# Causal attention in pairs of heads: the order of its work made by a list scheduler in the builder

## The chip, the core and the metric

The kernel runs on one core of a Trainium2 chip. The metric is the device time of one execution in microseconds; the profile is of one more execution of the same program. The core's engines each run their own queue in order and wait for one another by semaphores: TensorE (PE, matmuls and transposes), VectorE (DVE), ScalarE (ACT), GpSimd (POOL), and SyncE (SP), which here issues transfers.

## What is computed

Attention with a causal mask over 2 x 12 heads of 448 positions, then a gated layer (gate, value, output weights, float64 in memory), then eight experts of which each token uses one.

```python
scores = scale * np.matmul(q, k.transpose(0, 1, 3, 2))      # 2 x 12 heads, 448 x 448, head_dim 64
scores = np.where(mask, -1000000000.0, scores)               # causal
scores = scores - np.max(scores, axis=-1, keepdims=True)
attn = np.exp(scores)
attn = attn / (np.sum(attn, axis=-1, keepdims=True) + 1e-09)
x = np.matmul(attn, v)            # -> (896 tokens, 768)
xn = x / rms * rms_g
out1 = (silu(xn @ w_gate) * (xn @ w_val)) @ w_out
...                               # routing, then relu(x @ w1[e]) @ w2[e] for each token's expert
```

## The kernel before

The heads are taken in twelve pairs (NP = 12, n is the pair), so that two heads of 64 fill 128 partitions. The 448 positions are four chunks of 112 queries; chunk c sees (c+1) x 112 keys, so chunk 3 is the widest. For one pair the work is:

- keys and queries are loaded (`load_qk`, SP), transposed on PE (`prep_t`, L225, four transposes each) and copied out of PSUM (`prep_out`, keys on DVE L233, queries on ACT L231);
- `score` (L256, mask added by L258): chunks 0 and 1 into one PSUM tile, chunk 2 and chunk 3 each into another; there are two such tiles (`pss`);
- `rowmax` (DVE, L264), then `expo` (ACT, L270, one exponential for each head and chunk, which also sums the row);
- `invert` (DVE, L275 and L276: add and reciprocal), then `norm`: chunks 0 to 2 are scaled on POOL (L283), chunk 3 on ACT, one instruction for each head (L286);
- `trans` (L301): 20 transposes of the scaled probabilities in six groups through two PSUM tiles (`pst`), each group copied out (three groups of 4 on DVE, one of 4 and two of 2 on ACT) into one tile `pt` per head;
- `pv` (L316): the value product into `ps_x`; `xevac` copies it out on DVE (L323); `xhigh` (ACT, L328) and `xlow` (DVE, L333) make the two parts of the rounded result, `square` (ACT, L344) and `add_square` (POOL, L351) the sum of squares.

The order is written by hand: a loop over n in L499 to L593 issues, in each turn, the scores and exponentials of pair n, the transposes of pair n-1 and the value product's end of pair n-2, so each engine's queue holds them in just this order. Between them stand `chore` steps: single operations of the conversion of the first gate and value weights (float64 bits to a high and a low float32 part: `f64_ops`, DVE L144, L147, L150, ACT L154, DVE or POOL L156), eight halves in all. In the last two turns `ahead` puts products of the first weight slice (f=0) between. `warm` (L199) is a matmul with zeros; it stands only at the start. After the attention the gate and value products run (`products`, L457 to L459): twelve slices f, two batch halves each, 36 matmuls for one half. A slice needs its converted weights; the program does four halves of conversion for each further slice.

Of the kernel before, what the change touches and what calls it, by code (L numbers as in the profile page):

```python
# [31 lines left out]
E = 8  # L32
# [8 lines left out]
def build(ctx, tc, q, k, v, w_gate, w_val, w_out, rms_g, emb, tau, w1, w2, out, dbg=None):  # L41
# [196 lines left out]
    def begin(n):  # L238
        st[n] = {
            "ps": {}, "pt": {},  # L240
            "p": a2.tile([CP, 2, 10 * CP], F32, name="p", tag="p", bufs=2),
            "nm": a2.tile([CP, NCH, 2], F32, name="nm", tag="nm", bufs=3),
            "sm": a2.tile([CP, NCH, 2], F32, name="sm", tag="sm", bufs=3),
        }

    def score(n, cs):

        e = st[n]
        bank = pss.tile([P, 2, 512], F32, name="ps_s", tag="s")
        qt, kt = parts[n, "qn"], parts[n, "kn"]  # L250
# [15 lines left out]
    def expo(n, c):  # L266
        e = st[n]
        w = (c + 1) * CP
        for h in range(2):
            A.activation(e["p"][:, h, COLS[c]:COLS[c] + w], e["ps"][c][:, h, :], AF.Exp, bias=e["nm"][:, c, h:h + 1],  # L270
                         accum_out=e["sm"][:, c, h:h + 1])
# [6 lines left out]
    def norm(n, c):  # L278

        e = st[n]  # L280
        d = e["p"][:, :, COLS[c]:COLS[c] + (c + 1) * CP]
        if c < NCH - 1:
            G.tensor_mul(d, d, e["sm"][:, c, :].unsqueeze(2).to_broadcast([CP, 2, (c + 1) * CP]))  # L283
        else:
            for h in range(2):
                A.mul(d[:, h, :], d[:, h, :], e["sm"][:, c, h:h + 1])  # L286


    TOFF = [0, 4 * CP, 8 * CP, 7 * CP]

    def trans(n, h, bank):
        e = st[n]
        if bank == 0:
            e["pt"][h] = a2.tile([CP, 10 * CP], F32, name="pt", tag="pt", bufs=4)
        ps = pst.tile([P, 512], F32, name="ps_t", tag="t")
        base = bank * 4 * CP
        w = 0
        for kc in ((0,), (1, 3), (2,))[bank]:
            for c in range(kc, NCH):
                o = TOFF[kc] - base + (c - kc) * CP  # L300
                T.transpose(ps[:CP, o:o + CP], e["p"][:, h, COLS[c] + kc * CP:COLS[c] + (kc + 1) * CP],  # L301
                            ident[:CP, :CP])
                w = max(w, o + CP)
        return e["pt"][h][:, base:base + w], ps[:CP, :w]
# [4 lines left out]
    def pv(n, kcs):  # L309
        vn = qkv[n, "vn"]  # L310
        if kcs[0] == 0:
            xps[n] = tbank() if n == NP - 1 else psx.tile([P, 512], F32, name="ps_x", tag="x")
        for kc in kcs:
            w = (NCH - kc) * CP
            for h in range(2):
                T.matmul(xps[n][h * D:(h + 1) * D, kc * CP:S], vn[:, kc, h * D:(h + 1) * D],  # L316
                         st[n]["pt"][h][:, TOFF[kc]:TOFF[kc] + w], start=kc == 0, stop=kc == NCH - 1)

    xraw = {}

    def xevac(n):
        xraw[n] = a2.tile([P, S], F32, name="xraw", tag="xraw", bufs=3)
        V.tensor_copy(xraw[n], xps.pop(n)[:, :S])  # L323

    def xhigh(n):

        b, j = divmod(n, NPAIR)
        A.mul(xh[:, j, b * S:(b + 1) * S], xraw[n], gT[:, j:j + 1])  # L328

    def xlow(n):  # L330
        b, j = divmod(n, NPAIR)
        cols = slice(b * S, (b + 1) * S)
# [25 lines left out]

    def means(b):

        ps = tbank()
        for c in range(NCH):
            T.matmul(ps[:CP, c:c + 1], xsq[b][:, c * CP:(c + 1) * CP], ones[:, :1], start=True, stop=True)
        rms[b] = a1.tile([CP, NCH], F32, name="r", tag="r", bufs=2)
        V.tensor_scalar(out=rms[b], in0=ps[:CP, :NCH], scalar1=1.0 / DM, scalar2=1e-6, op0=ALU.mult, op1=ALU.add)
# [115 lines left out]

    with tc.manual_schedule():
        load_qk(0)
        load_qk(1)
        load_qk(2)
# [3 lines left out]
        begin(0)  # L489
        first2 = pss.tile([P, 2, 512], F32, name="ps_s", tag="s")  # L490
        for x, (nm, engine) in enumerate((("kn", A), ("qn", V))):
            prep_out(*prep_t(0, nm, first2[:, x, :]), engine)
            warm(bank, 2)
        score(0, (0, 1))
        for nm, engine in (("kn", A), ("qn", V)):
            prep_out(*prep_t(1, nm, tbank()), engine)
            warm(bank, 2)
        load_v(0)
        for n in range(NP + 2):  # L499
# [35 lines left out]
            elif n:  # L535
                chore()
# [748 lines left out]
```

## Time and profile before

| | |
|---|---|
| median of 3 runs | 680.58 us (678.58 to 683.65) |
| profiled execution | 681.85 us, span 680.1 us |
| busy over the span | PE 628.8, DVE 468.6, ACT 315.3, POOL 202.2 us |
| attention | about 4 to 175 us |
| gate and value products | to 343.9 us |
| granted clock, 40 slices of 17 us, tenths | 9989777797999999999999999979989999999999 |

A busy share is time in which an engine has an instruction under way. Matmuls overlap, so PE's share says little of how near it is to its limit; the distance between starts says more. The granted clock is TensorE's alone: 1.00 is 2.4 GHz, 0.50 is 1.2 GHz, and a number between is a mean over a stretch. A wait is put down to the engine that ended it. In the waits and the timeline a name such as `xl` is the tile that is written; `p` are the probabilities, `nm` the negated maxima, `sm` the row sums and their reciprocals.

### The profile page before, as it was taken

What the parts mean: (1) busy time and instruction counts of PE and PEld (TensorE: products, weight loads), DVE (VectorE), ACT (ScalarE), POOL (GpSimd) and SP (SyncE); (2) the same over time, 40 slices, a digit from 0 to 9 for tenths busy, and PEclk for the clock granted to TensorE, in tenths of its full rate; (3) what the DMA queues carried; (4) which work ended last, traced back from release to release, by engine and by line L of the source; (5) the groups of instructions that cost most, each with busy time, mean ns of one, the idle gap of its engine ahead of it and who ended that gap; (6) DMA issues with size and microseconds to landing.
All of it is one profiled execution on the core that took longest, in us unless ns stands there. A gap on an engine that the chain in (4) does not pass through costs nothing. (4 is left out here: it accounts for less than half of the span.)

```text
span 680.1 us, 10132 instructions
## 1 busy us (share of the span) xinstructions
PE 628.8 (92%) x3402; PEld 513.0 (75%) x3402; DVE 468.6 (69%) x848; ACT 315.3 (46%) x669; POOL 202.2 (30%) x198
## 2 busy tenths in 40 slices
PE   8889788879999999999999999978989898999996
PEld 4545455546899999999999999846768687888885
DVE  3676664565899999999658999667348687841431
ACT  2766665665422323322253223567347687741321
POOL 2322323133254444444303444013213313331100
PEclk9989777797999999999999999979989999999999
DMA  7731411000365555555168226328739989981100
GB/s 177 179 92 28 104 38 38 1 24 24 95 178 161 171 160 167 148 177 160 51 213 282 86 74 206 117 71 274 286 103 313 368 306 348 332 309 48 48 24 10
DMA packets 83664, 101.85 MB, mean 150 GB/s; under 512 B 38368, under 2 KB 62944, under 8 KB 83570
## 3 DMA queue, kind: packets, MB, share of 16 engines
q1 hardware_dynamic: 80704, 90.12, 42.6%
q0 software_dynamic: 1856, 7.87, 3.3%
q10 hardware_dynamic: 1010, 2.76, 1.0%
q8 instruction: 42, 0.69, 0.4%
q14 instruction: 52, 0.43, 0.2%
HBM read 95.19 MB, written 6.71 MB: 150 GB/s over the span
## 5 line engine op out<-in xcount | busy, mean ns | idle before, releaser
L283 POOL TENSOR_TENSOR p<-p,sm 112x224 f32<-112x224 f32 (+2 forms) x36 | 34.7, 992 | 82.1 <-DVE sm L276 77.2
L256 PE MATMUL ps_s<-knt,qnt 64*112 64x112 f32 (+3 forms) x192 | 41.9, 520 | 18.6 <-ACT p L270 18.6
L156 POOL TENSOR_TENSOR wl<-t,wh 128x384 fp32r<-128x384 f32 x40 | 42.7, 1078 | 54.5 <-ACT wh L154 54.5
L150 DVE SCALAR_TENSOR_TENSOR t<-raw,t 128x384 int32<-128x384 int32 x72 | 57.1, 794 | 1.8
L796 PE MATMUL ps_y<-wo,hh 128*128 128x384 f32 x168 | 58.0, 345 | 0.0
L797 PE MATMUL ps_y<-wo,hh 128*128 128x384 f32 x168 | 56.6, 337 | 0.0
L798 PE MATMUL ps_y<-wo,hlo 128*128 128x384 f32 x168 | 56.6, 337 | 0.0
L270 ACT ACTIVATE p<-ps_s,nm 112x112 f32<-112x112 f32 (+3 forms) x96 | 46.1, 496 | 20.8 <-DVE nm L264 20.8
L457 PE MATMUL ps_g<-xh,wh 128*128 128x448 f32 x144 | 53.6, 372 | 0.0
L459 PE MATMUL ps_g<-xh,wl 128*128 128x448 f32 x144 | 53.5, 372 | 0.0
L458 PE MATMUL ps_g<-xl,wh 128*128 128x448 f32 x144 | 53.0, 368 | 0.0
L457 PE MATMUL ps_v<-xh,wh 128*128 128x448 f32 x144 | 52.8, 367 | 0.0
L459 PE MATMUL ps_v<-xh,wl 128*128 128x448 f32 x144 | 52.6, 365 | 0.0
L458 PE MATMUL ps_v<-xl,wh 128*128 128x448 f32 x144 | 52.6, 365 | 0.0
L147 DVE SCALAR_TENSOR_TENSOR t<-raw,t 128x384 int32<-128x384 int32 x72 | 50.4, 700 | 1.5
L154 ACT CAST wh<-t 128x384 fp32r<-128x384 f32 x48 | 24.7, 514 | 52.8 <-DVE t L150 44.3
L264 DVE TENSOR_REDUCE nm<-ps_s 112x2 f32<-112x224 f32 (+3 forms) x48 | 34.2, 733 | 17.5 <-PE ps_s L258 17.4
L301 PE MATMUL ps_t<-ident,p 112*112 112x112 f32 x240 | 41.2, 310 | 2.9 <-ACT pt L564 2.9
L256 PEld LDWEIGHTS ps_s<-knt,qnt 64*112 64x112 f32 x192 | 15.8, 206 | 33.4 <-ACT p L270 21.2
L144 DVE TENSOR_SCALAR t<-raw 128x384 int32<-128x384 int32 x72 | 38.0, 528 | 3.7 <-POOL wl L156 3.7
L156 POOL TENSOR_TENSOR wo<-t,wo 128x384 fp32r<-128x384 f32 x24 | 25.7, 1071 | 35.9 <-ACT wo L154 35.9
L301 PEld LDWEIGHTS ps_t<-ident,p 112*112 112x112 f32 x240 | 29.1, 160 | 7.7 <-ACT pt L564 5.7
(298 smaller groups left out, 1649.6 us busy)
## 6 DMA issues: line engine op xcount, KB each, us to landing
r<-in_moe_w SPq DMA_DIRECT2D x78, 384.0 KB, 5.3
hB<-in_moe_w SPq DMA_DIRECT2D x29, 384.0 KB, 3.4
raw<-in_moe_w_gate SPq DMA_DIRECT2D x24, 384.0 KB, 4.0
raw<-in_moe_w_val SPq DMA_DIRECT2D x24, 384.0 KB, 3.2
raw<-in_moe_w_out SPq DMA_DIRECT2D x24, 384.0 KB, 3.2
onehot<-in_moe_w SPq DMA_DIRECT2D x13, 384.0 KB
hA<-in_moe_w SPq DMA_DIRECT2D x8, 384.0 KB, 3.1
kn<-in_k SPq DMA_DIRECT2D x24, 112.0 KB, 2.5
```

The costliest lines, as they stand in the source:

```text
L147: V.scalar_tensor_tensor(out=t, in0=w[:, :, 1], scalar=-0x40000000, in1=t, op0=ALU.bitwise_and, op1=ALU.bitwise_or)
L150: V.scalar_tensor_tensor(out=t, in0=w[:, :, 0], scalar=29, in1=t, op0=ALU.logical_shift_right, op1=ALU.bitwise_or)
L156: low.tensor_sub(lo, f, hi.bitcast(F32))
L256: T.matmul(bank[:CP, h, o:o + w], qt[rows, c * CP:(c + 1) * CP], kt[rows, :w], start=True, stop=False)
L270: A.activation(e["p"][:, h, COLS[c]:COLS[c] + w], e["ps"][c][:, h, :], AF.Exp, bias=e["nm"][:, c, h:h + 1], accum_out=e["sm"][:, c, h:h + 1])
L301: T.transpose(ps[:CP, o:o + CP], e["p"][:, h, COLS[c] + kc * CP:COLS[c] + (kc + 1) * CP], ident[:CP, :CP])
L457: T.matmul(pg[:, :S], ah, bh, start=j == 0, stop=False)
L458: T.matmul(pg[:, :S], ah, bl, start=False, stop=False)
L459: T.matmul(pg[:, :S], al, bh, start=False, stop=j == NJ - 1)
L796: T.matmul(o, hh, bh, start=f == 0, stop=False)
L797: T.matmul(o, hh, bl, start=False, stop=False)
L798: T.matmul(o, hl, bh, start=False, stop=f == NF - 1)
```

## The change

The loop is replaced by a planner in the builder, `attention_order`. It lists every step of every pair as a node with an engine, a duration written in the code, the nodes that it needs, the buffers that it takes and gives, and a place from a table of constants. It then places one node after another: of the nodes that could start earliest on their engine (within 0.12) the one with the smallest place. The result is one list; the program issues it in that order, and where the plan leaves PE idle over 0.35 us it puts up to four `warm` matmuls into the PSUM tile that the next step writes. The conversions (`ch0` to `ch4`) and the early products (`gv`) are nodes too, with the largest places.

Besides the order: chunk 3 is scaled on POOL with the others; the first transposed group is copied by ACT for both heads (before by DVE for the first head), so ACT has four groups and DVE two; the transposed probabilities have a tile for each group (`pt0`, `pt1`, `pt2`, four of each) in place of one per head; `ps_x` is not copied out, `xhigh`, `square` and `xlow` read PSUM; scores and exponentials of chunk 1 come ahead of chunk 0, and chunk 3 ahead of chunk 2. Loads of keys and queries are issued four pairs ahead, of values five, the first of them in one row at the start.

```diff
     def norm(n, c):
 
         e = st[n]
-        d = e["p"][:, :, COLS[c]:COLS[c] + (c + 1) * CP]
-        if c < NCH - 1:
-            G.tensor_mul(d, d, e["sm"][:, c, :].unsqueeze(2).to_broadcast([CP, 2, (c + 1) * CP]))
-        else:
-            for h in range(2):
-                A.mul(d[:, h, :], d[:, h, :], e["sm"][:, c, h:h + 1])
+        w = (c + 1) * CP
+        d = e["p"][:, :, COLS[c]:COLS[c] + w]
+        G.tensor_mul(d, d, e["sm"][:, c, :].unsqueeze(2).to_broadcast([CP, 2, w]))
...
-    def xevac(n):
-        xraw[n] = a2.tile([P, S], F32, name="xraw", tag="xraw", bufs=3)
-        V.tensor_copy(xraw[n], xps.pop(n)[:, :S])
...
-        A.mul(xh[:, j, b * S:(b + 1) * S], xraw[n], gT[:, j:j + 1])
+        A.mul(xh[:, j, b * S:(b + 1) * S], xps[n][:, :S], gT[:, j:j + 1])
...
+    PLACES = dict(Pk=24, KE=12, Pq=19, QE=25, S01=10, S2=18, S3=-10, M0=21, E00=21, E01=5, M1=-7, E10=0, E11=-9,
...
+    def attention_order():
...
+            add("Pk", n, T, .385, [], ["pm", "kt"])
...
+            add("S01", n, T, 1.2, own("KE", "QE"), ["pss"])
+            add("S3", n, T, 1.08, own("S01"), ["pss"])
+            add("S2", n, T, .9, own("S3"), ["pss"], ["kt", "qt"])
...
+            for c, weight in enumerate((.56, .93, 1.6, 2.1)):
+                add(f"N{c}", n, G, weight, own("R1" if c < 3 else "R2"))
...
+                    add(f"C{h}{b}", n, V if b == 1 else A, (.53, .62, .34)[b], own(f"T{h}{b}"), gives=["pst"])
...
+            picks = []
+            for e, l in first.items():
+                t0 = min(l)[0]
+                picks.append(min((place[k], t, k) for t, k in l if t <= t0 + .12))
+            _, t, k = min(picks, key=lambda x: (x[1], x[0], x[2]))
...
-        for n in range(NP + 2):
-            cur, old = n < NP, 1 <= n <= NP
-            x = n - 2 if n >= 2 else None
...
+        for (kind, n), gap in attention_order():
+
+            fill = min(4, int((gap - .1) / .22)) if gap > .35 else 0
...
```

What this does to ACT's queue is seen in one pair in the middle of the attention. Before (L270 exponentials, `p,sm`; L538, L564, L572 copies of transposed groups; L286 scaling of chunk 3; L328 high part; L231 queries; L344 square):

```order
L270 ACTIVATE p,sm<-ps_s,nm 112x112 x2
L270 ACTIVATE p,sm<-ps_s,nm 112x224 x2
L270 ACTIVATE p,sm<-ps_s,nm 112x336 x2
L538 COPY pt<-ps_t 112x224
L270 ACTIVATE p,sm<-ps_s,nm 112x448 x2
L564 COPY pt<-ps_t 112x448
L286 ACTIVATE p<-p,sm 112x448 x2
L328 ACTIVATE xh<-xraw,gT 128x448
L572 COPY pt<-ps_t 112x224
L231 ACTIVATE qnt<-tq 128x448
L344 ACTIVATE sq<-xraw 128x448
```

In the changed program (L266 exponentials, L638 copies, L335 square, L320 high part; the number in `pt_` is that of a tile):

```order
L266 ACTIVATE p,sm<-ps_s,nm 112x224
L231 ACTIVATE qnt<-tq 128x448
L266 ACTIVATE p,sm<-ps_s,nm 112x224
L266 ACTIVATE p,sm<-ps_s,nm 112x112
L266 ACTIVATE p,sm<-ps_s,nm 112x448
L266 ACTIVATE p,sm<-ps_s,nm 112x112
L266 ACTIVATE p,sm<-ps_s,nm 112x448
L638 COPY pt_1005<-ps_t 112x224
L335 ACTIVATE sq<-ps_x 128x448
L320 ACTIVATE xh<-ps_x,gT 128x448
L638 COPY pt_1027<-ps_t 112x448
L266 ACTIVATE p,sm<-ps_s,nm 112x336
```

The scaling L286 is gone, square and high part stand behind one short copy, and the exponentials of the widest chunk (448) alternate with those of the narrowest (112), ahead of those of the 336 keys.

On DVE, before, from the copy of the value product on (L323), with L565 a transposed copy, L275 and L276 the sums and reciprocals of chunk 3, L333 the low part, L264 the maxima of the next pair:

```order
L323 COPY xraw<-ps_x 128x448
L233 COPY knt<-tq 128x448
L150 SCALAR_TENSOR_TENSOR t<-raw,t 128x384
L565 COPY pt<-ps_t 112x448
L275 TENSOR_SCALAR sm<-sm 112x2
L276 RECIPROCAL sm<-sm 112x2
L333 SCALAR_TENSOR_TENSOR xl<-xraw,gT,xh 128x448
L156 TENSOR_TENSOR wl<-t,wh 128x384
L264 TENSOR_REDUCE nm<-ps_s 112x2 x2
```

In the changed program (L638 transposed copies, L271 and L272 reciprocals, L259 maxima, L325 low part, L233 keys):

```order
L233 COPY knt<-tq 128x448
L638 COPY pt_1012<-ps_t 112x448
L271 TENSOR_SCALAR sm<-sm 112x2
L272 RECIPROCAL sm<-sm 112x2
L259 TENSOR_REDUCE nm<-ps_s 112x2
L638 COPY pt_1037<-ps_t 112x448
L325 SCALAR_TENSOR_TENSOR xl<-ps_x,gT,xh 128x448
L259 TENSOR_REDUCE nm<-ps_s 112x2
L271 TENSOR_SCALAR sm<-sm 112x6
L272 RECIPROCAL sm<-sm 112x6
L259 TENSOR_REDUCE nm<-ps_s 112x2
```

The copy out of PSUM is gone; one maximum stands between the reciprocals of chunk 3 (`112x2`) and the low part, and the reciprocals of the other chunks (`112x6`) come only after the next pair's first maximum.

On PE, before, the end of one turn: transposes of pair n-1, the last three parts of the value product of pair n-2, transposes, chunk-3 scores:

```order
L301 MATMUL ps_t<-ident,p 112x112 x4
L316 MATMUL ps_x<-pt,vn 64x336 x2
L316 MATMUL ps_x<-pt,vn 64x224 x2
L316 MATMUL ps_x<-pt,vn 64x112 x2
L301 MATMUL ps_t<-ident,p 112x112 x4
L256 MATMUL ps_s<-knt,qnt 112x448 x2
```

In the changed program the whole value product (L314; one line for each head) is a block directly behind the chunk-3 scores, with the key transposes of a later pair (L225) in its middle; from its first part to the chunk-2 scores (L251, 336 keys):

```order
L314 MATMUL ps_x<-pt_1027,vn 64x448
L314 MATMUL ps_x<-pt_1061,vn 64x448
L225 MATMUL tq<-ident,kn 128x112 x4
L314 MATMUL ps_x<-pt_1012,vn 64x336
L314 MATMUL ps_x<-pt_1037,vn 64x336
L314 MATMUL ps_x<-pt_1005,vn 64x224
L314 MATMUL ps_x<-pt_1073,vn 64x224
L314 MATMUL ps_x<-pt_1012,vn 64x112
L314 MATMUL ps_x<-pt_1037,vn 64x112
L292 MATMUL ps_t<-ident,p 112x112 x6
L251 MATMUL ps_s<-knt,qnt 112x336 x2
```

## Rows read from the trace of the kernel before

**Rows 1.** Stretches: busy us (x instructions) of PE, PEld, DVE, ACT, POOL; clock, DMA share, GB/s.
```profile
13.40:47.50 34.10, 28.65 (x206) 15.98 (x205) 23.09 (x47) 23.66 (x81) 8.26 (x9) 1.00 0.62 149
44.10:47.50 3.40, 1.42 (x10) 0.76 (x11) 2.16 (x5) 2.69 (x12) 0.00 (x0) 1.00 0.63 166
47.50:54.40 6.90, 6.90 (x35) 4.36 (x33) 3.12 (x8) 3.94 (x10) 2.72 (x3) 0.51 0.16 36
47.50:160.20 112.70, 96.73 (x566) 58.60 (x565) 68.90 (x141) 69.30 (x208) 35.98 (x35) 0.77 0.16 41
182.80:343.90 161.10, 161.10 (x800) 148.97 (x798) 145.32 (x243) 45.12 (x85) 67.49 (x64) 1.00 0.51 148
```

**Rows 2.** Timeline: start, us, engine, line, operation, names, count. Chunk-3 scores; first f=1 product.
```profile
16.53 1.01 PE L256 MATMUL ps_s<-knt,qnt 64*112 64x448 f32 x4 [0.40 <-ACT p L270]
...
33.89 1.01 PE L256 MATMUL ps_s<-knt,qnt 64*112 64x448 f32 x4
...
150.29 1.84 PE L256 MATMUL ps_s<-knt,qnt 64*112 64x448 f32 x4 [2.14 <-ACT p L270]
...
182.76 0.36 PE L457 MATMUL ps_g<-xh,wh 128*128 128x448 f32 x1
```

**Rows 3.** Waits, 30 to 150 us: waiter <- releaser: us in total, times, longest.
```profile
DVE xl L333 <- ACT xh L328: 17.3, 9, 1.9
...
ACT p L270 <- DVE nm L264: 15.8, 18, 2.6
PE ps_s L256 <- ACT p L270: 14.7, 8, 2.8
ACT p L286 <- DVE sm L276: 13.0, 10, 2.0
```

**Rows 4.** Timeline, weight loads on PE in two periods at full clock (28 to 48 us).
```profile
32.08 1.14 PEld L316 LDWEIGHTS ps_x<-pt,vn 112*64 112x64 f32 x12
...
33.36 0.38 PEld L301 LDWEIGHTS ps_t<-ident,p 112*112 112x112 f32 x4
...
36.93 0.77 PEld L301 LDWEIGHTS ps_t<-ident,p 112*112 112x112 f32 x8
...
38.30 0.43 PEld L225 LDWEIGHTS tq<-ident,qn 112*128 112x128 f32 x4
...
38.87 0.20 PEld L316 LDWEIGHTS ps_x<-pt,vn 112*64 112x64 f32 x4
...
39.77 0.28 PEld L256 LDWEIGHTS ps_s<-knt,qnt 64*112 64x112 f32 x4 [0.70 <-issue]
...
40.62 0.38 PEld L301 LDWEIGHTS ps_t<-ident,p 112*112 112x112 f32 x4
```

**Rows 5.** Groups by line and shape, 14 to 160 us: busy us, mean ns | idle before.
```profile
L283 POOL TENSOR_TENSOR p<-p,sm 112x672 f32<-112x672 f32 x12 | 17.0, 1420 | 0.0
...
L286 ACT ACTIVATE p<-p,sm 112x448 f32<-112x448 f32 x24 | 14.8, 662 | 14.6 <-DVE sm L276 14.6
...
L283 POOL TENSOR_TENSOR p<-p,sm 112x448 f32<-112x448 f32 x12 | 11.9, 996 | 0.0
...
L515 DVE COPY pt<-ps_t 112x448 f32<-112x448 f32 x11 | 6.8, 615 | 2.0 <-PE ps_t L301 2.0
...
L147 DVE SCALAR_TENSOR_TENSOR t<-raw,t 128x384 int32<-128x384 int32 x6 | 5.2, 869 | 0.0
```

**Rows 6.** Timeline, 175 to 185 us: a bit operation alone, a table load, both engines together.
```profile
175.87 0.55 DVE L147 SCALAR_TENSOR_TENSOR t<-raw,t 128x384 int32<-128x384 int32 x1
...
179.04 1.28 ACT L626 ACT_TABLE_LOAD   x1
...
183.96 1.02 POOL L156 TENSOR_TENSOR wl<-t,wh 128x384 fp32r<-128x384 f32 x1 [1.04 <-ACT wh L154]
...
184.12 1.27 DVE L147 SCALAR_TENSOR_TENSOR t<-raw,t 128x384 int32<-128x384 int32 x1
```

**Rows 7.** Timeline: the seven warm-up matmuls at the start.
```profile
1.06 3.17 PE L199 MATMUL ps_x<-zerob 128*128 128x512 bf16 x7 [1.06 <-DVE zerob L66]
```

More of the change, by code (lines that the diff above doesn't have):

```diff
@@ L236, in build, with score @@
     st = {}
[L238 to L248, printed above, removed]
+    def score(n, cs, fill):
+        e = st.setdefault(n, {"ps": {}, "pt": {}})
+        if cs[-1] == 0:
+            e["nm"], e["sm"] = (a2.tile([CP, NCH, 2], F32, name=x, tag=x, bufs=3) for x in ("nm", "sm"))
         bank = pss.tile([P, 2, 512], F32, name="ps_s", tag="s")
+        warm(bank[:, 0, :], fill)
         qt, kt = parts[n, "qn"], parts[n, "kn"]
@@ L292, in trans @@
+    GROUPS = ((0,), (1, 3), (2,))
+    def trans(n, h, b, fill):
         e = st[n]
-        if bank == 0:
-            e["pt"][h] = a2.tile([CP, 10 * CP], F32, name="pt", tag="pt", bufs=4)
         ps = pst.tile([P, 512], F32, name="ps_t", tag="t")
-        base = bank * 4 * CP
-        w = 0
-        for kc in ((0,), (1, 3), (2,))[bank]:
+        warm(ps, fill)
+        o = 0
+        for kc in GROUPS[b]:
+            w = (NCH - kc) * CP
             for c in range(kc, NCH):
[L300 to L303, printed above, removed]
@@ L304, in trans, with ptrans @@
-        return e["pt"][h][:, base:base + w], ps[:CP, :w]
+                T.transpose(ps[:CP, o + (c - kc) * CP:o + (c - kc + 1) * CP],
+                            e["p"][:, h, COLS[c] + kc * CP:COLS[c] + (kc + 1) * CP], ident[:CP, :CP])
+            e["pt"][h, kc] = b, o, w
+            o += w
+        t = a2.tile([CP, o], F32, name=f"pt{b}", tag=f"pt{b}", bufs=4)
+        e["pt"][h, b, "tile"] = t
+        return t, ps[:CP, :o]
+    def ptrans(n, h, kc):
+        b, o, w = st[n]["pt"][h, kc]
+        return st[n]["pt"][h, b, "tile"][:, o:o + w]
@@ L357, in tbank, with means_products, means_sums @@
         return pst.tile([P, 512], F32, name="ps_t", tag="t")
-    def means(b):
[L361 to L365, printed above, removed]
+    mean_ps = {}
+    def means_products(b):
+        mean_ps[b] = tbank()
+        for c in range(NCH):
+            T.matmul(mean_ps[b][:CP, c:c + 1], xsq[b][:, c * CP:(c + 1) * CP], ones[:, :1], start=True, stop=True)
+    def means_sums(b):
+        rms[b] = a1.tile([CP, NCH], F32, name="r", tag="r", bufs=2)
+        V.tensor_scalar(out=rms[b], in0=mean_ps[b][:CP, :NCH], scalar1=1.0 / DM, scalar2=1e-6, op0=ALU.mult,
+                        op1=ALU.add)
+    def means(b):
+        means_products(b)
+        means_sums(b)
     def roots(b):
@@ L486, in build @@
+    with tc.manual_schedule():
+        for n in range(3):
+            load_qk(n)
+        load_v(0)
+        SY.dma_start(out=itau, in_=tau.to_broadcast([P, 1]))
+        SY.dma_start(out=en, in_=emb)
+        SY.dma_start(out=gT, in_=rms_g.rearrange("(j p) -> p j", p=P))
+        load_qk(3)
+        load_v(1)
+        for _ in range(2):
+            fetch_raw()
+        for n in range(2, 5):
+            load_v(n)
         A.mul(zero1, zero1, 0.125)
@@ L594, in build @@
         ahead(100)
-        add_square()
         means(1)
```

287 lines of the change are left out of this document (159 added, 128 removed).

## Prediction

> **What bounds the kernel now.** I read the slices of the page first. TensorE (PE) is busy all through, but from 40 to 160 us its clock line moves between 5 and 9 while every other engine is at 4 to 7 tenths: a stretch in which no engine is full. That is the attention, twelve head pairs. Then I took stretches. From 47.5 to 160.2 us PE counts 96.7 busy of 112.7 us, but at a mean granted clock of 0.77; DVE 68.9, ACT 69.3, POOL 36.0 [rows 1]. From 182.8 to 343.9 us, the gate and value products, PE is busy without a gap at full clock: eleven slices of 72 matmuls, 0.203 us each. That stage is bound by PE, and starting it earlier moves all that follows.
>
> The beat of the attention is the distance between the widest score products (chunk 3, 448 keys; I call them S3). They start at 16.53 for pair 0, 33.89 for pair 2, 150.29 for pair 11 [rows 2]: nine pairs in 116.4 us, 12.93 us a pair. The first matmul of the second slice of the products (f=1) starts at 182.76; this is the mark that I use for the end.
>
> What a pair costs PE at full clock I take from starts in a stretch at 1.00 (13.4 to 47.5 us [rows 1]). S3, two transposes, a key transpose group and both small score products: 33.89 to 36.93, 3.04 [rows 2, 4]. Eight transposes 0.77, ten more at the same 0.096 each 0.96. Query transposes 0.57 (38.30 to 38.87), first part of the value product 0.90 (to 39.77), chunk-2 scores 0.85 (to 40.62), the rest of the value product 1.28 (32.08 to 33.36) [rows 4]. Sum 8.37 us. So PE could turn a pair in 8.4 and takes 12.9: 4.5 us go to waiting, some of it paid as clock.
>
> The waits say who holds whom. In 120 us ACT waits 13.0 us for DVE's reciprocal before it scales chunk 3, DVE then 17.3 for ACT's high part of the value product (which stands on ACT behind that scaling), ACT 15.8 for row maxima (which stand on DVE behind the low part), PE 14.7 for a score bank that the exponentials hold [rows 3]. It is a ring through the written order; no engine is its bound. After such a wait the clock falls: in 44.1 to 47.5 PE was busy 1.42 of 3.40 us, and the next 6.9 us ran at 0.51, the lower level, 1.2 GHz [rows 1].
>
> **The change, part by part.**
> *Order.* PE now runs S3, the whole value product, transposes and next scores in one block. DVE's low part still stands ahead of the next pair's maxima, but the high part that it waits for stands on ACT behind a short copy and a square, no longer behind the scaling of chunk 3, which is POOL's; and the exponentials of chunk 3 alternate with those of chunk 0. If that takes the ring apart, what remains is each engine's load per pair (from rows 1 divided by 8.71 pairs of 12.93 us):
> - PE 8.37, unchanged but for a few warm-up matmuls at the ends.
> - ACT 69.3/8.71 = 7.95, less the two scalings of chunk 3 (2 x 0.662), plus one transposed copy taken from DVE (unseen on ACT under that shape in these rows; at most DVE's 0.615) [rows 5]: 7.25. High part and square now read PSUM; ACT's other PSUM reads of the kind are in the same sum, so I cost that at nothing.
> - DVE 68.9/8.71 = 7.91, less that copy and the copy of the value product out of PSUM (same kind and size, 0.615 each) [rows 5]: 6.7.
> - POOL 36.0/8.71 = 4.13, plus chunk 3. The trace has no such row: the step from 448 to 672 elements costs 0.424, so 896 cost 1.85; if the price per element does not fall, 1.420 x 896/672 = 1.89 [rows 5]. 1.85 taken: 6.0.
>
> *POOL beside DVE.* POOL's share of a pair goes from 0.32 to about 0.63. A DVE bit operation that takes 0.55 alone took 1.27 when a POOL subtraction had begun 0.16 us before it [rows 6], and in the attention the mean of this line is 0.869 [rows 5]: 0.32 more, at a POOL share of 0.32. Twice the share means about twice that, on three such operations per conversion and 0.7 conversions per pair: some 0.7 us more than DVE now pays, 7.4. From above, both pairs of small reciprocal operations are also held for half a POOL instruction (0.7 us each): 8.8.
> The Trainium skill says the same more sharply ("SBUF — State Buffer", section "SBUF: two separate sides"): DVE and GpSimd share a port pair as an exclusive lock, and the loser waits for the whole instruction. It speaks against giving POOL more work. The 1.27 agrees (0.55 plus what was left of POOL's 1.02). By it alone every held operation waits its full rest, DVE stands at the 8.8, the period at the 10.5 below, and the time would be 650.
>
> *The period.* From below 8.4 (PE never waits). From above 10.5: DVE 8.8 plus the wait for maxima that ACT shows now, 15.8 us in 120, or 1.7 a pair [rows 3]. ACT at 7.25 fits into either with little room, and the widest maximum has to land between two exponentials; so I take the middle, 9.5. Nine pairs: 9 x (12.93 - 9.5) = 30.9 us.
>
> *The start.* Pair 0's S3 moves ahead of pair 1's query transposes. Against that, four more warm-up matmuls stand ahead of the first transposes (seven take 3.17, so 1.8 us [rows 7]) and four behind them, on a bank that must be copied first. S3 then starts between 8.5 and 16.5; I take 12.5. Two periods without a value product bring S3 of pair 2 at 7 each (they took 8.7) to 26.4: 7.5 us ahead, between 4 and 10. The loads are queued further ahead on SP, three value pairs more in front of the fifth pair's keys and queries, and the transposes that want these move from 38.30 [rows 4] to about 25. No row says when they would land; coming late by 3 us is in the lower end.
>
> *The end.* From S3 of pair 11 to the mark now 182.76 - 150.29 = 32.5. After, PE has there by its order: S3 1.04, three value products of 0.90 + 1.28, 40 transposes 3.84, chunk 2 0.85, 72 products 14.6, fills and small matmuls 2.2: 29.1 if nothing waits. The last pair's maxima, POOL scaling and copies can't all hide; 31.5 taken, 1.0 gained, between -1.5 and 3.4. Two more table loads on ACT (1.28 each [rows 6]) lie beside the products; uncovered they are the 2.6 of the lower bound.
>
> *After the mark* nothing is changed: 0. PE had no gap there.
>
> Sum: 7.5 + 30.9 + 1.0 = 39.4. The profiled execution took 681.85 (span 680.1), 1.3 above the median 680.58: 681.85 - 39.4 = 642.4, and against the median **641**.
>
> **Rivals.**
> 1. *The clock still falls once a pair.* If one wait of the old size stays, 6.8 us run at 1.2 GHz. At that level S3 of pair 11 took 1.84, at full clock S3 of pair 2 took 1.01 [rows 2], a factor 1.82, so 6.8 x (1 - 1/1.82) = 3.1 us of PE work are lost: period 8.4 + 3.1 = 11.5, gain 7.5 + 12.9 + 1, time 659. For it: the page's clock line falls again and again from 47 us on. Against: the falls followed waits that the new order takes apart.
> 2. *The plan does not fit the chip.* The order is made from durations written in the builder; it has 0.385 for a group of preparing transposes that takes 0.57, and 2.1 for chunk 3 on POOL against 1.85. In an in-order queue every misfit is a wait. At 12.5 a pair, 668; at the old 12.9, 672.
> 3. *The gain is given back.* In the products stage DVE is busy 145.3 of 161.1 us [rows 1]. If the weight conversions of the third slice came late, PE would wait for at most four halves of about 2 us: 649. Against: the order has the eight early conversions ahead of the products, as before.
> 4. *Slower: the attention stays at 1.2 GHz.* Then PE needs 8.37 x 1.82 = 15.2 a pair: 9 x 2.3 lost, about 8 more in the tail's transposes and value products, 8.5 won at the ends: 701. It decides from a mean period of 13.9 on (12.93 + 8.5/9). Against it stands the very stretch in which PE is most dense in transposes and small matmuls, 33.89 to 40.62, which lies in a stretch at 1.00 throughout [rows 1, 2, 4].
> The Trainium skill speaks for this one ("TensorE: Matmul & The Clock Gate", Part 4): full clock does not engage for transposes. The full-clock stretch disagrees for this mixture of transposes and matmuls.
>
> **How the numbers follow.** Forecast (period 8.4 to 10.5) 0.71; clock 0.15; plan 0.05; given back 0.06; slower 0.03. The forecast's own span, with all terms at their ends, is 627 to 656 (period 8.4, start 10, end 3.4; period 10.5, start 4, end -1.5). The range, 630 to 661, leaves out the luckiest end of the forecast and cases 2 and 4. A measurement of this kernel tells about 1% from no change: faster by more 0.94 (a part of case 2 is within 1.5%), within 1% 0.03, slower 0.03.
>
> **What would show it.** Right: S3 starts 9 to 10 us apart at a granted clock near 1.00 from 20 us on; the ACT wait for the reciprocal and the DVE wait for the high part gone from the waits; first f=1 product near 143. POOL's 896-element scaling near 1.85; DVE's three bit operations longer in the mean than 0.869. Wrong: PE waits of 2 us a pair and clock falls (case 1); S3 distances over 12 at full clock (case 2); PE gaps behind the mark (case 3).

## The result and the profile after

The changed kernel takes 644.98 us (median of 4 runs, 643.63 to 646.08) against 679.58 us for the kernel before (4 runs, 675.35 to 683.65): ratio 0.949, 95% interval 0.943 to 0.955. Measured again later on another chip it took 642.69 us (6 runs) against 681.95: 0.943 (0.939 to 0.947). Forecast were 641 us, 630 to 661.

The profiled execution took 644.0 us. Of its page, the span, PE's share and the granted clock in 40 slices of 16 us:

```profile
span 642.3 us, 10154 instructions
...
PE 608.7 (95%) x3409; PEld 500.4 (78%) x3409; DVE 451.5 (70%) x824; ACT 308.8 (48%) x659; POOL 232.9 (36%) x210
...
PEclk9899998899999999999999999979999899999999
```

The 7s that stood in the fifth to tenth slice of before are gone; two dips, the 8s in the second and seventh slice, are left in the attention. The timeline has the beat: chunk-3 scores of pairs 0, 2, 10 and 11, and the mark, the first matmul of the second weight slice (columns as in [rows 2]).

```profile
10.33 1.01 PE L251 MATMUL ps_s<-knt,qnt 64*112 64x448 f32 x4
...
29.34 1.01 PE L251 MATMUL ps_s<-knt,qnt 64*112 64x448 f32 x4
...
100.73 1.01 PE L251 MATMUL ps_s<-knt,qnt 64*112 64x448 f32 x4
...
114.96 1.84 PE L251 MATMUL ps_s<-knt,qnt 64*112 64x448 f32 x4
...
149.44 0.36 PE L453 MATMUL ps_g<-xh,wh 128*128 128x448 f32 x1
```

From pair 2 to 10 the distance is 71.4 us in eight pairs, 8.9 each, where [rows 2] have 12.9. The last distance is 14.2, and the score at 114.96 takes 1.84 us in place of 1.01: half clock. The mark came from 182.76 to 149.44, 33.3 us. Stretches (columns as in [rows 1]):

```profile
24.80:106.70 81.90, 79.29 (x612) 47.71 (x610) 66.82 (x139) 67.02 (x214) 57.05 (x42) 1.00 0.37 93
106.70:117.00 10.30, 9.74 (x42) 5.72 (x42) 4.05 (x10) 4.86 (x15) 4.66 (x5) 0.50 0.25 75
...
149.40:310.50 161.10, 161.10 (x800) 149.00 (x799) 139.29 (x239) 44.47 (x86) 65.74 (x62) 1.00 0.50 145
...
29.30:100.70 71.40, 71.14 (x550) 42.88 (x548) 58.08 (x121) 59.53 (x189) 49.64 (x39) 1.00 0.37 94
100.70:115.00 14.30, 11.38 (x63) 6.75 (x62) 8.91 (x18) 7.48 (x25) 8.93 (x5) 0.71 0.19 56
```

In the eight even pairs PE is busy 71.1 of 71.4 us at full clock, and the 8.9 us of a pair lie near the 8.37 that the prediction counted from starts: the attention is now close to PE's bound. By engine a pair costs DVE 7.3, ACT 7.4, POOL 6.2 us. The products take the same 161.1 us as before. The waits from 30 to 100 us (columns as in [rows 3], 70 us here for 120 there):

```profile
DVE nm L259 <- PE ps_s L253: 6.3, 15, 1.0
...
ACT p L266 <- DVE nm L259: 3.7, 8, 0.9
PEld tq L225 <- ACT qnt L231: 3.5, 5, 0.7
```

None of the four waits of [rows 3] is left at its size: the exponentials' wait for maxima fell from 15.8 (1.7 a pair) to 3.7 (0.5 a pair), the other three do not appear.

**The 14.2 us.** In the stretch of 100.70 to 115.00 PE waits once for 2.9 us, for POOL (waits, 98 to 118 us):

```profile
PE ps_t L292 <- POOL p L279: 2.9, 1, 2.9
```

The groups of POOL by shape, from 101 to 107 us and, for an even pair, from 56 to 60.9 (columns as in [rows 5]):

```profile
L279 POOL TENSOR_TENSOR p<-p,sm 112x448 f32<-112x448 f32 x1 | 4.0, 3995 | 0.0
...
L279 POOL TENSOR_TENSOR p<-p,sm 112x448 f32<-112x448 f32 x1 | 0.9, 931 | 0.0
```

The same scaling takes 0.93 us at one place and 4.00 at the other. What DVE does beside the long one (timeline; the scaling runs from 102.31 to 106.30):

```profile
102.01 1.09 DVE L259 TENSOR_REDUCE nm<-ps_s 112x2 f32<-112x896 f32 x1 [0.31 <-PE ps_s L253]
103.02 0.55 DVE L156 TENSOR_TENSOR wl<-t,wh 128x384 fp32r<-128x384 f32 x1
103.48 0.62 DVE L144 TENSOR_SCALAR t<-raw 128x384 int32<-128x384 int32 x2
104.02 1.02 DVE L147 SCALAR_TENSOR_TENSOR t<-raw,t 128x384 int32<-128x384 int32 x2
104.96 0.55 DVE L150 SCALAR_TENSOR_TENSOR t<-raw,t 128x384 int32<-128x384 int32 x1
105.43 0.90 DVE L271 TENSOR_SCALAR sm<-sm 112x2 f32<-112x2 f32 x1
106.24 0.55 DVE L150 SCALAR_TENSOR_TENSOR t<-raw,t 128x384 int32<-128x384 int32 x1
```

Six conversion operations (L156, twice L144, twice L147, L150) follow one another without a gap, each at its undisturbed length, and POOL ends 0.8 us after the sixth. Two halves are converted there in turn (x2). One of them is not in the plan: it belongs to the third weight slice, whose code stands behind the planned part, and the rest of the program's ordering put it there.

### The profile page after: what moved, and what is told of

The parts are those of the page before. It is cut to its first block, busy times and chain, and to the rows that moved or that the text cites. A ratio compares the mean times of both kernels' runs of the same rounds, so it can differ in the third digit from the quotient of the medians.

```text
span 642.3 us, 10154 instructions
## 1 busy us (share of the span) xinstructions
PE 608.7 (95%) x3409; PEld 500.4 (78%) x3409; DVE 451.5 (70%) x824; ACT 308.8 (48%) x659; POOL 232.9 (36%) x210
## 5 line engine op out<-in xcount | busy, mean ns | idle before, releaser
L279 POOL TENSOR_TENSOR p<-p,sm 112x896 f32<-112x896 f32 (+3 forms) x48 | 66.0, 1394 | 44.6 <-DVE sm L272 28.8
L156 POOL TENSOR_TENSOR wl<-t,wh 128x384 fp32r<-128x384 f32 x40 | 42.0, 1071 | 54.7 <-ACT wh L154 51.4
L266 ACT ACTIVATE p<-ps_s,nm 112x112 f32<-112x112 f32 (+3 forms) x96 | 46.7, 493 | 12.9 <-DVE nm L259 12.4
L144 DVE TENSOR_SCALAR t<-raw 128x384 int32<-128x384 int32 x72 | 43.5, 605 | 10.5 <-POOL wl L156 9.5
L150 DVE SCALAR_TENSOR_TENSOR t<-raw,t 128x384 int32<-128x384 int32 x72 | 48.5, 673 | 1.8
L259 DVE TENSOR_REDUCE nm<-ps_s 112x2 f32<-112x448 f32 (+3 forms) x48 | 35.0, 734 | 20.8 <-PE ps_s L253 18.3
L147 DVE SCALAR_TENSOR_TENSOR t<-raw,t 128x384 int32<-128x384 int32 x72 | 47.5, 661 | 1.6
L156 POOL TENSOR_TENSOR wo<-t,wo 128x384 fp32r<-128x384 f32 x24 | 25.7, 1073 | 35.1 <-ACT wo L154 35.1
L292 PE MATMUL ps_t<-ident,p 112*112 112x112 f32 x240 | 34.3, 274 | 3.6 <-POOL p L279 2.9
L251 PE MATMUL ps_s<-knt,qnt 64*112 64x224 f32 (+3 forms) x192 | 37.3, 468 | 0.0
L1053 POOL DMA_INDIRECT hB<-ydram,idx x13 | 14.8, 1142 | 58.1 <-DVE lg L956 22.8
L154 ACT CAST wo<-t 128x384 fp32r<-128x384 f32 x24 | 12.3, 513 | 46.0 <-DVE t L150 46.0
```

Source lines behind the costliest of these rows:

```text
L144: V.tensor_scalar(out=t, in0=w[:, :, 1], scalar1=3, scalar2=0x3FFFFFFF, op0=ALU.logical_shift_left, op1=ALU.bitwise_and)
L147: V.scalar_tensor_tensor(out=t, in0=w[:, :, 1], scalar=-0x40000000, in1=t, op0=ALU.bitwise_and, op1=ALU.bitwise_or)
L150: V.scalar_tensor_tensor(out=t, in0=w[:, :, 0], scalar=29, in1=t, op0=ALU.logical_shift_right, op1=ALU.bitwise_or)
L156: low.tensor_sub(lo, f, hi.bitcast(F32))
```

## The experiments

Theory A is that of the prediction: the written order forms a ring of waits, and taking it apart is the gain. Against it stand that the edits did it (POOL's scaling above all), that the clock did it, and that any order made by a planner would do. Theory P says that the 14.2 us come from POOL being held off by DVE's pile. Each ratio is against the kernel before, run beside it on the same chip. "Distance" is the mean from pair 2 to pair 11 in the profiled execution, clock the granted one in that stretch.

| kernel | median us | ratio (95%) | distance | clock | mark |
|---|---|---|---|---|---|
| before | 679.6 | 1 | 12.93 | 0.82 | 182.8 |
| changed | 645.0 | 0.949 (0.943-0.955) | 9.51 | 0.95 | 149.4 |
| hand_all | 681.0 | 0.994 (0.991-0.998) | 13.18 | 0.84 | 183.1 |
| hand_warm | 673.2 | 0.989 (0.983-0.996) | 11.86 | 1.00 | 173.0 |
| hand_xl | 667.4 | 0.982 (0.977-0.987) | 10.95 | 0.97 | 163.4 |
| n3_act | 659.5 | 0.964 (0.958-0.970) | 10.20 | 1.00 | 158.7 |
| flat | 663.3 | 0.974 (0.967-0.981) | 11.75 | 0.98 | 166.4 |
| spread_hold | 656.0 | 0.962 (0.955-0.969) | 10.63 | 1.00 | 157.2 |
| hold | 638.7 | 0.937 (0.930-0.943) | 8.94 | 1.00 | 142.5 |
| hold_nofill | 644.2 | 0.945 (0.939-0.950) | 8.94 | 1.00 | 144.1 |

**Edits without the order.**

```diff
 kernel before
-        if c < NCH - 1:
-            G.tensor_mul(d, d, e["sm"][:, c, :].unsqueeze(2).to_broadcast([CP, 2, (c + 1) * CP]))
-        else:
-            for h in range(2):
-                A.mul(d[:, h, :], d[:, h, :], e["sm"][:, c, h:h + 1])
+        G.tensor_mul(d, d, e["sm"][:, c, :].unsqueeze(2).to_broadcast([CP, 2, (c + 1) * CP]))
...
-        xraw[n] = a2.tile([P, S], F32, name="xraw", tag="xraw", bufs=3)
-        V.tensor_copy(xraw[n], xps.pop(n)[:, :S])
+        xraw[n] = xps.pop(n)[:, :S]
...
-                V.tensor_copy(*trans(n - 1, 0, 0))
+                A.copy(*trans(n - 1, 0, 0))
...
+            if x is not None:
+                square(x)
             if old:
                 pv(n - 1, (0,))
-            if x is not None:
-                square(x)
```

> The kernel before with its hand-written order and the other edits of the change: chunk 3 scaled on POOL, the value product read in PSUM, the first transposed group copied by ACT. Theory A (the order is the cause): ACT no longer waits for the reciprocal (13.0 us in 120), but DVE's low part still stands ahead of the next maxima and behind ACT's high part, so the period falls from 12.9 to 12 at most: 671 (662 to 680). Rival B (the edits are the cause): two thirds of the gain or more, 657 or less.

Measured 0.994: half a per cent, and in the profile nothing (mark 183.1 against 182.8). The waits from 30 to 150 us:

```profile
ACT p L270 <- DVE nm L264: 29.3, 18, 5.0
...
PE ps_x L312 <- ACT sq L339: 14.0, 7, 2.3
```

The wait for the reciprocal is gone with the scaling, but the exponentials wait for maxima longer than before (29.3 against 15.8 [rows 3]), and PE has a new wait of 14.0: the value product's one PSUM tile is now held until ACT has squared it. DVE's operations have also grown longer beside POOL's new scaling (groups of DVE by shape, 30 to 150 us):

```profile
L275 DVE TENSOR_SCALAR sm<-sm 112x2 f32<-112x2 f32 x9 | 9.6, 1069 | 0.0
L156 DVE TENSOR_TENSOR wl<-t,wh 128x384 fp32r<-128x384 f32 x5 | 8.6, 1729 | 0.0
L150 DVE SCALAR_TENSOR_TENSOR t<-raw,t 128x384 int32<-128x384 int32 x5 | 7.5, 1499 | 0.1
L147 DVE SCALAR_TENSOR_TENSOR t<-raw,t 128x384 int32<-128x384 int32 x6 | 7.1, 1182 | 0.0
```

In the kernel before the same four take 0.31, 0.70, 0.66 and 0.87 us there. With L144 (0.82 for 0.45) that is some 20 us more on DVE in 120, or 2.2 a pair, and the maxima stand in DVE's queue behind it. So rival B falls: these three edits, in the written order, buy nothing. The theory's own number (671) was too good by 10. How much of that is the held PSUM tile and how much is DVE's longer operations was not taken apart. The change's other edits (a tile for each transposed group, the order of the chunks, the earlier loads) were not tried in the written order.

**One step of the written order moved.**

```diff
 kernel before
                 rowmax(n, 0), rowmax(n, 1)
+                if n >= 3:
+                    xlow(n - 3)
                 expo(n, 0), expo(n, 1)
...
-            if x is not None:
-                xlow(x)
             if n:
                 chore()
```

> The kernel before with one step moved: DVE's low part of the value product stands one turn later, behind the first two maxima of the next pair instead of ahead of them. Theory (the ring goes DVE low part <- ACT high part <- ACT scaling <- DVE reciprocal, and the maxima behind the low part): this cuts the link, the wait of the low part (1.9 us at most) no longer delays the maxima, the period falls from 12.9 to about 11.3: 680 - 15 = 665 (660 to 670). Rival (another link takes over at once, such as the wait of the scaling for the reciprocal, which the edits alone did not shorten either): period 12.5 or more, 676 or more.

Measured 0.982, distance 10.95, expected 11.3. Waits from 30 to 132 us:

```profile
ACT p L270 <- DVE nm L264: 7.0, 12, 1.0
DVE xl L333 <- ACT xh L328: 2.2, 5, 0.6
```

17.3 and 15.8 in [rows 3] have become 2.2 and 7.0. One moved instruction a pair gives 1.98 of the 3.42 us of distance that the change gave: the link that I read in the waits was the right one. The other two waits of [rows 3] stay (14.9 for ACT's scaling, 10.3 for the score bank). The clock rose from 0.82 to 0.97 with the move; its part in the 1.98 is not separated.

**The clock held, the order kept.**

```diff
 kernel before
+                if 2 <= n:
+                    warm(pm.tile([P, 512], F32, name="wq", tag="misc"), 10)
                 score(n, (3,))
```

> The kernel before, with ten warm-up matmuls (2.2 us at full clock) in front of the chunk-3 scores of pairs 2 to 11, into the PSUM tile of the key and query transposes: they stand where PE waits 2.2 to 2.8 us for the exponentials. Theory A (the ring of the written order binds, through ACT and DVE; the clock comes second): the clock stays up, but the distance falls only by what PE's slow work adds to the ring, to 11.5 to 12: 680 - 10 = 670 (664 to 676). Rival (the clock is the cost): with it held the distance falls by the 3.1 us that half clock takes from PE, to 9.8: 680 - 28 = 652.

The clock is 1.00 from 4.7 to 144.6 us, the distance 11.86, the time 0.989. Stretch of the pairs 2 to 11:

```profile
33.70:140.40 106.70, 101.58 (x703) 56.36 (x702) 76.33 (x148) 70.52 (x217) 34.82 (x34) 1.00 0.20 50
```

In pairs 3 to 11 the weight load behind the warm-ups still waits for ACT, 0.5 to 1.1 us, so they stand in the wait and hardly delay the scores. So of 12.93 us the falling clock accounts for 1.1, not for the 3.1 of the rival, which is the loss of a pair with 6.8 us at half clock. By the mean clock of 0.82 a pair has 4.7 us at half clock and its PE work loses an estimated 2.1: about half of that lay where PE would have waited anyway. Theory A's numbers hold (11.5 to 12; 664 to 676).

**Other plans.** n3_act puts chunk 3 back on ACT (two instructions, 1.3 us in the plan); flat sets all places of the table to 0; spread_hold is told below. Each plan is made anew.

```diff
 n3_act
...
-            for c, weight in enumerate((.56, .93, 1.6, 2.1)):
-                add(f"N{c}", n, G, weight, ...
+            for c, weight in enumerate((.56, .93, 1.6, 1.3)):
+                add(f"N{c}", n, G if c < 3 else A, weight, ...
 flat
-            place[k] = 10 * n + PLACES[kind] if at is None else at
+            place[k] = 10 * n if at is None else at
```

> The changed kernel, but chunk 3 is scaled on ACT as before (one step of 1.3 us in the plan, two instructions), the plan made anew. Theory A (the written order's ring was the cause, any order without it does): ACT rises to 8.6 us a pair, still under 9.3; period 8.9 to 9.5, time 645 + 9 x 0.5 = 650 (646 to 655). Rival B (moving the scaling to POOL took the ring apart): the period is over 11 again, 645 + 9 x 2.3 = 666 or more.

> The changed kernel with every step's place in the table set to 0, so that of the steps that can start the one of the earliest pair goes first; edits, buffers and durations as in the change. Theory (a plan beats the written order only where its table fits the chip; ACT-scaled chunk 3 and strewn conversions made plans with 10.7 and 10.3 us a pair at full clock): period 10 to 11, 645 + 9 x 1.6 = 659 (654 to 668). Rival (any order without the ring will do): period 9, 645.

n3_act's distance is 10.2, expected 8.9 to 9.5; its time of 659 lies between the two theories (655 and 666). Its stretch, pairs 2 to 11:

```profile
34.60:126.40 91.80, 85.80 (x644) 50.58 (x642) 67.56 (x137) 74.10 (x229) 35.90 (x34) 1.00 0.30 79
```

ACT has 8.2 us a pair, PE 9.5 counted busy, and neither fills 10.2, at full clock. flat, with the same steps as the changed kernel, needs 11.75, more than the theory's 10 to 11; its time of 663 lies inside the 654 to 668. Its DVE has 8.7 us a pair where the changed kernel's has 7.4: L147 takes 1.00 and L150 1.09 there, for 0.62 and 0.61. A list scheduler with the change's edits, but without the table, takes a third of the 3.42 us (12.93 to 11.75); the table of places brings the rest. What is due to POOL's scaling and what to a table that was fitted with it cannot be told from n3_act, since table and edit belong together.

**The pile at pair 10.** hold queues the conversions of the third slice on DVE behind the low part of pair 10.

```diff
 changed kernel (`lows` holds the low parts' instructions)
+            with tc.issue_after(lows[NP - 2].ins) if f == 1 else ExitStack():
                 if b == 0:
                     gv[f + 1] = [gv_conv(w_gate, f + 1)]
 spread_hold, besides
             t += weight + (.35 if e is T else .3 if k[0][0] == "E" else .1)
+            if k[0][:2] == "ch":
+                t += 1.4
```

> The changed kernel, but the first conversions of the third weight slice are queued on DVE behind the low part of pair 10 (in the changed kernel two of their halves stand among the last two pairs of the attention, three bit operations of one of them interleaved with those of the planned half). Theory (POOL held off): in the changed kernel the scaling of 448 elements of pair 10 took 4.00 us on POOL, 0.93 in other pairs, while DVE ran seven bit operations of 0.35 to 0.55 us one behind the other; PE then waited 3.1 us and the clock fell. With three of the seven gone that scaling should take 2.5 to 3, the wait fall to about 1.5; the time falls by 1.5 us to 643.5, by up to 5 (640) if the clock then stays up. Rival (the plan's end is badly ordered, whoever runs beside it): the scaling is long because its inputs or its queue are late, nothing moves, 645.

> As hold, and in the plan each step of a conversion is followed by 1.4 us in which the next may not start, so the bit operations are strewn over the pairs. Theory (POOL held off): no scaling of 448 elements takes over 2.2 us, the distance of the last two chunk-3 scores falls from 14.2 to about 9.3, the clock stays at 1.00 to the products: 645 - 5 = 640, 638 to 642. Rival (the plan's end): distance and clock stay, 645; a second rival: strewn operations hold POOL a little in every pair, the period rises by 0.3 and eats 3 us of it, 643.

With hold the distances are 8.6 to 9.2 throughout, the last 9.1, the clock does not fall between 7 and 409 us, and the mark stands at 142.51. Its stretch, its 448-element scaling at pair 10, and DVE beside it:

```profile
28.90:109.40 80.50, 79.08 (x611) 47.50 (x609) 65.46 (x135) 66.78 (x213) 56.82 (x44) 1.00 0.35 90
...
L279 POOL TENSOR_TENSOR p<-p,sm 112x448 f32<-112x448 f32 x1 | 2.3, 2319 | 0.0
...
102.61 0.55 DVE L156 TENSOR_TENSOR wl<-t,wh 128x384 fp32r<-128x384 f32 x1
103.07 0.35 DVE L144 TENSOR_SCALAR t<-raw 128x384 int32<-128x384 int32 x1
103.46 1.17 DVE L147 SCALAR_TENSOR_TENSOR t<-raw,t 128x384 int32<-128x384 int32 x1
104.66 0.80 DVE L150 SCALAR_TENSOR_TENSOR t<-raw,t 128x384 int32<-128x384 int32 x1
```

POOL gets in behind the second operation (L147 then waits and takes 1.17), the scaling takes 2.32 in place of 4.00, PE's wait falls from 2.9 to 1.2, and the clock stays at 1.00. Theory P holds. The strewn plan failed: its scores stand 4.4 to 18.1 us apart at a clock of 1.00 throughout. Neither of my theories foresaw it; a constant that was to delay forty small steps made the planner place all the others anew.

Changed kernel and hold once more, side by side:

> The changed kernel unchanged, beside hold_again on one chip, for the interval of what hold gains: 645, against the kernel before 0.949.

> Kernel hold unchanged. The mark of the second weight slice moved from 149.4 to 142.5 with it; what lies behind the mark differs from run to run by some us. Theory: 6.9 us faster than the changed kernel, 638; rival (its gain lay in the part behind the mark and was chance): within 2 us of the changed kernel.

Ratios 0.943 (0.939 to 0.947) and 0.940 (0.936 to 0.944), medians 642.69 and 640.09. The mark stands again at 149.19 and 142.48, and again the long scaling took 3.99, so the 6.7 to 6.9 us up to there are seen in both pairs of profiles. Of the whole time 2.6 us are seen here, inside the intervals, neither the 6.9 of the theory nor the rival's under 2; between the medians of all runs it is 3.7 (9 of hold 640.06, 10 of the changed kernel 643.8). The part behind the products took 330.8 and 336.8 us in the two profiles of hold, 331.8 and 333.8 in those of the changed kernel; whether hold gives something back there stays open.

**Piles made on purpose**, in kernel hold, at the place where POOL scales. The diff is that of piles (`latest[3]` is the PSUM tile of the last chunk-3 scores); chains has eight of the two-source operations at pair 3, on two spare tiles in turn, and eight at pair 7 on one. Each of the two kernels was executed once.

```diff
 hold
+        if n == 3:
+            for _ in range(5):
+                V.scalar_tensor_tensor(out=spare[0], in0=spare[1], scalar=-0x40000000, in1=spare[0],
+                                       op0=ALU.bitwise_and, op1=ALU.bitwise_or)
+        elif n == 6:
+            for _ in range(3):
+                V.tensor_reduce(out=spare[0].bitcast(F32)[:CP, :2], in_=latest[3], axis=AX.X, op=ALU.max, negate=True)
+        elif n == 8:
+            for _ in range(8):
+                V.tensor_scalar(out=spare[0], in0=spare[1], scalar1=3, scalar2=0x3FFFFFFF,
+                                op0=ALU.logical_shift_left, op1=ALU.bitwise_and)
```

> Kernel hold with three extra piles of DVE work on spare data, each put into DVE's queue where POOL scales the 448-element chunks of a pair (0.93 us undisturbed): at pair 3 five bit operations with two sources in SBUF (2.75 us), at pair 6 three maxima read from PSUM (3.3 us), at pair 8 eight bit operations with one source in SBUF (2.8 us). Theory (POOL is held while DVE runs operations on SBUF): at pair 3 the scaling takes about 3.7 us, at pair 6 about 1.0 though DVE is just as busy; for the one-source operations the rows say nothing, 1 to 3.7. The distance of the chunk-3 scores grows by 2 to 4 us at pair 3, and there by the DVE delay alone at pair 6. Rival (POOL is late since DVE's queue is late): the scaling keeps its 0.93 to 1.5 in all three, and the pairs grow alike. In the program's order the spare operations use numbers that change no output.

> Kernel hold with eight spare bit operations with two sources in SBUF put into DVE's queue at two places: at pair 3 as two chains that alternate (each waits only for the one but last, as in the changed kernel at pair 10), at pair 7 as one chain (each waits for the last). Theory (POOL gets in only in the gap that a chain leaves): at pair 3 the scaling that meets the pile takes its own time and 3 us or more, at pair 7 its own time and about 1. Rival (the pile's length decides): both take the same, own time and 1 to 2. The spare numbers change no output.

At pair 6 the maxima from PSUM leave POOL alone, as expected; groups of POOL there, then those of chains at pair 3:

```profile
L298 POOL TENSOR_TENSOR p<-p,sm 112x448 f32<-112x448 f32 x1 | 0.9, 930 | 0.0
...
L289 POOL TENSOR_TENSOR p<-p,sm 112x448 f32<-112x448 f32 x1 | 1.2, 1247 | 0.0
L289 POOL TENSOR_TENSOR p<-p,sm 112x224 f32<-112x224 f32 x1 | 0.9, 869 | 0.0
```

At pair 3 of piles the scaling took 2.03 (expected 3.7), at pair 8, beside one-source operations, 1.95. In chains both kinds of pile cost POOL the same 0.32 on each scaling, and DVE's first operations took 1.24, 1.28 and 0.91: the two engines took turns. So the expectation that two chains starve POOL and one does not fell, and with it the reason I gave for the 4.00. That SBUF operations on DVE hold POOL off, and PSUM reads (at pair 6) do not, stands; what decides who goes next stays open. Where POOL's scaling begins does not decide it alone: at pairs 3 and 8 of piles it also began while DVE was in a maximum with the pile behind it (at 48.53 and 97.28 us), and took 2.03 and 1.95. In these two and in hold, POOL got in at an operation that began 0.03 to 0.04 us after the end of the one ahead; at pair 10 of the changed kernel each of the six began before the one ahead had ended. In chains, at pair 3, there is no such gap either, but POOL was inside the scaling ahead of it when the pile came, and took its turn. A pile without gaps that meets the scaling's start inside a maximum, as at pair 10, was not made on purpose.

The piles cost time whether POOL was held or not: the distance behind the pile of pair 3 is 11.6, of pair 6 (POOL undisturbed) 11.0, of pair 8 12.5, instead of 8.8, 9.0 and 9.2, and 16.6 and 17.6 in chains, where the pile stood ahead of the widest maximum. A fallen clock is part of the last three (0.87 at pair 8 of piles, 0.72 and 0.73 in chains). At pair 6 the delay of DVE's queue alone costs 2.0 us, at pair 3 both delays together 2.8.

**Without the planner's warm-ups.**

```diff
 hold
-            fill = min(4, int((gap - .1) / .22)) if gap > .35 else 0
+            fill = 0
```

> Kernel hold without the planner's warm-up matmuls (27 of them before 24 us, three behind 120). Theory (they keep the clock up at the start, where PE waits for loads): without them the clock falls once or twice before 30 us, the score of pair 2 moves from 28.9 to 30, the attention behind it keeps its 8.8 and full clock: hold + 1 to + 3. Rival (they cost what I charged them, 1.8 us and a bank): hold - 1 to - 2. A second rival: the attention needs them to reach full clock at all: hold + 10 or more.

The planner's warm-ups are 27 in all. Without them the score of pair 2 comes at 30.64 instead of 28.93, the clock falls from 23.7 to 30.5, and then stays at 1.00 until 406 us with the same 8.94 a pair: the mark is 1.6 us later, within the theory's 1 to 3. The median is 5.5 us later; the profiled execution has 7 us more behind the products, which no warm-up touches, so I count only the 1.6.

## Why the prediction was right, and where it was not

**What bounded the kernel.** Right. hand_all excludes three of the edits as a cause by themselves, hand_xl shows the link, hand_warm shows the clock to be the smaller part. Two readings of the page were off, and no term rests on them: from 40 us on its slices have the clock at 7 to 9, not 5 to 9 (the 0.51 of [rows 1] is a shorter stretch), and POOL at 1 to 3 tenths, not 4 to 7.

**Period, 9.5 (8.4 to 10.5).** The mean is 9.51, by luck: eight distances of 8.9 and one of 14.2. My middle stood for DVE paying for POOL's greater share. In this order it did not: the three bit operations, which I expected above their mean of 0.869 (L147 [rows 5]), took 0.62, 0.61 and 0.55 (L147, L150, L156, 29 to 115 us); POOL's 448 elements went from 0.996 [rows 5] to 1.77, 1.49 without the long one ((9 x 1.772 - 3.995)/8). In other orders DVE did pay: in hand_all (1.18, 1.50 and 1.73 for L147, L150 and L156, DVE at 9.4 us a pair, above my 8.8) and in flat. So the term was real, and the order decided who paid it; I had not foreseen that. ACT (7.4 for 7.25), DVE (7.3 for 6.7 to 7.4) and POOL (6.2 for 6.0) came as summed, the new scaling at 1.69 for 1.85. The loads left room, and the period went to PE's bound: 8.37 summed, 8.9 with the short waits at the query tile and behind weight loads. With the pile gone (hold) it is 8.94.

**The port rule.** The Trainium skill ("SBUF — State Buffer", section "SBUF: two separate sides") was weighed as a reason for 10.5 and 650. That the lock excludes the other engine for a whole instruction agrees: 1.24 us for DVE's 0.55 in chains, 1.17 in hold. By that section of the Trainium skill the engine that starts first gets the pair; this does not fit pair 10, where POOL's scaling had begun at 102.31 and DVE's L156, at 103.02, still took its 0.55. I had taken DVE for the loser: in this kernel it is mostly POOL, and a run of DVE operations made its 0.93 into 4.00.

**Start, 7.5 (4 to 10).** 4.55 (33.89 to 29.34). The first score came earlier than I took it (10.33 for 12.5), but the two periods without a value product took 8.9 and 10.1 for my 7 each; in hold 8.9 and 8.6. In hold the clock did not fall there; in the changed kernel it stood at 0.50 from 21.4 to 24.8 us. I priced them by PE, but in the waits of 4 to 30 us PE stands for DVE and ACT, four times, each time at a warm-up matmul:

```profile
PE tq L199 <- DVE knt L233: 1.9, 2, 1.2
PE ps_s L199 <- DVE itau L389: 0.9, 1, 0.9
PE tq L199 <- ACT qnt L231: 0.6, 1, 0.6
```

Twelve of the planner's warm-ups stand between the scores of pairs 0 and 2; with the waits right behind them they take 3.6 of PE's 19.0 us, and my two periods had none. Taking all warm-ups out does not gain that back (hold_nofill needs 20.1 us there, 6.8 of them at half clock). DVE has 5.8 and ACT 6.2 us of work a period there (7.3 and 7.4 in an even pair), the expert norm (`itau`) among it. That cause is read from the rows, not tested. The loads, of which I was afraid, end no wait of PE there.

**End, 1.0 (-1.5 to 3.4).** -2.0: from the last chunk-3 score to the mark 34.5 us, outside the bounds. 0.8 of it is the score at half clock; hold, at full clock, still needs 33.1. The failed step is the count of PE's work, 29.1: in hold PE is busy 32.4 of these 33.1 us, so it was not waits that I had left out. Counted from start to start there, the 72 products take 16.7 us (0.232 each, where I took the 0.203 of the products stage; here they stand between transposes), the 40 transposes 4.9 for 3.84, and the rest 0.9 more than I had.

**After the mark, 0.** The products took 161.1 us as before. Behind them the profiled execution was 4.5 shorter (336.3 to 331.8); with one kernel giving 330.8 and 336.8 there, this is no effect that I can claim. The sum at the mark, 39.4 forecast, is 33.3; the median moved by 34.6.

**The rivals.** 1 (clock falls every pair): no; two falls, 3.4 and 10.3 us long. 2 (the plan does not fit the chip): at one place, pair 10, by work that the plan does not contain; three other plans show how real it is, at 10.2 to 11.75 a pair. I gave it 0.05, too little for an order whose margin is half a microsecond. 3 (given back in the products): no; the stage is as long as before. 4 (attention at half clock): no; hold_nofill keeps 1.00 for 375 us, the attention among them, with no warm-up matmul in it. The rule of the Trainium skill behind it ("TensorE: Matmul & The Clock Gate", Part 4) disagrees with these rows as it did with those of before.

## What to carry to other kernels

Where no engine is full, look in the waits for a ring (each of a few waits of equal size released by the next), and try to move the one instruction that closes it before anything is rewritten: here that alone gave over half of the beat's gain. A machine-made order is as good as its numbers: feed it every operation that will run in its stretch, and after any edit read the beat anew, since a changed engine, constant or table gave 10.2, 10.6 and 11.75 us a pair where the fitted plan gives 8.9. When work moves from one engine to another, compare the lengths of both engines' operations before and after: beside POOL's new scaling DVE's grew in one order and not in the other. If one pair in twelve is long, compare the same instruction's duration there and elsewhere before looking for a late input.

## What the hardware showed that I had not expected

- A POOL multiplication of 0.93 us took 4.00 (3.99 when measured again) beside DVE operations on SBUF that followed one another without a gap; three PSUM maxima of 1.09 us beside it changed nothing (0.930). In chains the two engines took turns, 0.3 us lost on each POOL instruction and 0.4 to 0.7 on DVE's; in piles the same multiplication lost 1.0 to 1.1.
- The same two engines in the written order (hand_all): DVE's bit operations took 1.18 to 1.73 us, for 0.66 to 0.87 before, and POOL's 448-element multiplication 1.10.
- Half clock cost the old order 1.1 us a pair, where PE's work alone loses an estimated 2.1: work that is slowed in front of a wait costs only what the wait does not hide.
- In hold_nofill, transposes and small matmuls with no warm-up among them kept the granted clock at 1.00 from 30.5 us on, through 80 us of attention.
